# K pages and weights on one DMA queue, V pages on another, in a two-layer decode kernel

## The chip, the cores and the metric

The kernel runs on one core of one Trainium2 chip. The metric is the device time of one launch in microseconds (us), the median of several runs. Times inside an execution come from one profiled execution, taken by the hardware profiler, and are counted from the start of its span.

## What is computed

One token passes through two identical layers, each an attention block and a gated feed-forward block with residuals. The weights and caches of both layers are the same tensors, so the second layer reads them again. In short:

```python
W = 4096                                            # window: last 4096 of 32768 positions
q = (layernorm(x) @ wq)                             # 640 -> 32 heads x 192
scores = einsum("bhqd,bhkd->bhqk", q, k[-W:]) * 192 ** -0.5
x = x + einsum("bhqk,bhkd->bhqd", softmax(scores), v[-W:]) @ wo
y = layernorm(x)
x = x + (silu(y @ w1) * (y @ w3)) @ w2              # 640 -> 1536 -> 640
# and the same four lines once more
```

All data are bf16. Each head has its own K and V, so one head's window is 4096 x 192 elements, 1536 KB of K and as much of V.

## The kernel before

**Pages and slots.** All large data pass through one arena in on-chip memory (`arena`), cut into 16 slots (`NSLOT`) of 128 partitions x 6144 elements, 1536 KB each. One slot holds one page: a head's K window, a head's V window, a fifth of wq, or a part of wo, w1, w3 or w2.

**The list of loads.** The list `loads` (lines 147 to 172) is written out before anything runs. For each layer it holds five wq pages (`q`); then, for step i from 0 to 41, the V page of head number i - 10 and the K page of head number i, where these exist (`LEAD` is 10); then six entries for wo (`o`), which are 8 transfers, and four for the feed-forward weights (`fa` to `fd`). So the first ten K pages stand alone, then V and K alternate, and the last ten V pages stand alone. Heads go in four blocks of 8 (`HB`); their order is `ORDER`, other in the second layer than in the first. 13 K pages of the first layer (`RETAIN`) keep their slots and are not loaded again in the second layer.

**Who issues.** `refill` (line 174) takes entries off the list while a slot is free and issues their transfers at line 181, all on SP's queue (`nc.sync`). `done` (line 186) gives a page's slot back and calls `refill`. Both run while the program is being written: a transfer's place in the program is right behind the matmuls that were the last to read the slot it goes into, and `pin` keeps that order on each engine. An engine runs its instructions in the order of the program. The transfer waits for those matmuls and, as the semaphores go, for the landing of an earlier transfer. In all, 64 V pages, 51 K pages and 41 transfers of weights go this way. One small load, the input `xb` (line 75), is issued on ACT's queue before.

**One step of the attention** (`attention`, from line 407). Step i first takes V page i - 10 (`v_page`: 16 matmuls into `o_ps`), then K page i (`k_page`: two in-place transposes on DVE at line 262, then 12 matmuls into `s_ps`; a retained K page is not transposed again). PE takes these strictly in this order. ACT and the other engines do the following around blocks:

- before a block's first K page, `build_w` copies the block's q into `wst` with two copies on ACT (line 249) and two on POOL (line 251)
- after a block's last K page, `softmax_head`: the maximum on DVE (lines 274 to 283), `tb` on ACT (line 284), a transpose on DVE, the exp on ACT (line 289), a transpose on DVE (line 292)
- two steps later, `softmax_place`: five copies on ACT and three on DVE into `ptm` (line 302), which the V matmuls of the block read
- after the first V page of the next block, `combine`: a copy on ACT (line 321), two pairs of matmuls, and three operations on DVE that end in `otd`

**After the attention**, `wo_proj` multiplies `otd` by wo (96 small matmuls into `y_ps`), `y_to_residual` adds the result to x (from line 208), `layernorm` follows (from line 191), and `ffn` computes gate (`g_ps`), up (`u_ps`), silu and the product with w2. All matmuls carry line 72, the line of the helper `mm`. The last instruction is the store of `ob` (line 443).

Of the kernel before, what the change touches and what calls it, by code (L numbers as in the profile page):

```python
# [40 lines left out]
def kernel(  # L41
# [13 lines left out]
    nc = tc.nc  # L55
# [11 lines left out]
    def pin(ins):  # L67
        tc.keep_in_program_order(ins)
        return ins
# [104 lines left out]
    def refill():  # L174
        while free and loads:
            key, parts = loads.pop(0)
            s = free.pop(0)
            home[key] = s
            for off, n, src in parts:
                dst = arena[:, s * PGW + off:s * PGW + off + n] if off is not None else keep[:]  # L180
                pin(nc.sync.dma_start(out=dst, in_=src))  # L181

    def page(key):
        return arena[:, home[key] * PGW:home[key] * PGW + PGW]
# [1 line left out]
    def done(key):  # L186
        free.append(home.pop(key))
        refill()
# [218 lines left out]
    def attention(layer):  # L407
# [27 lines left out]
        wo_proj(layer)  # L435

    refill()
    ob = cst.tile([P, NCH], BF16, name="ob")
    for layer in range(2):
# [34 lines left out]
```

## Time and profile before

| what | value |
|---|---|
| median of 3 runs | 542.88 us (542.79 to 543.05) |
| profiled execution, its time | 548.4 us |
| profiled execution, its span | 546.6 us |
| bytes moved | 224.34 MB, mean 410 GB/s |
| SP's queue | 22608 packets, 223.98 MB |
| ACT's queue | 144 packets (`xb`) |
| mean granted TensorE clock | 0.668 of full speed |
| 0 to 280 us | 419 GB/s, DMA busy share 1.00 |
| 280 to 334 us | 381 GB/s, DMA busy share 0.96 |
| 334 to 541 us | 417 GB/s, DMA busy share 1.00 |

PE is TensorE's matmul row, PEld its weight loads, DVE is VectorE, ACT is ScalarE, POOL is GpSimd, SP is SyncE. A "q" behind an engine's name (SPq) stands for its sequencer, which issues transfers. Rows of groups give the line, engine, operation and the names written and read; rows of a timeline begin with start and duration in us. The chain is the work that ended last, followed back from the last instruction: at each step to what released it.

### The profile page before, as it was taken

What the parts mean: (1) busy time and instruction counts of PE and PEld (TensorE: products, weight loads), DVE (VectorE), ACT (ScalarE), POOL (GpSimd) and SP (SyncE); (2) the same over time, 40 slices, a digit from 0 to 9 for tenths busy, and PEclk for the clock granted to TensorE, in tenths of its full rate; (3) what the DMA queues carried; (4) which work ended last, traced back from release to release, by engine and by line L of the source; (5) the groups of instructions that cost most, each with busy time, mean ns of one, the idle gap of its engine ahead of it and who ended that gap; (6) DMA issues with size and microseconds to landing.
All of it is one profiled execution on the core that took longest, in us unless ns stands there. A gap on an engine that the chain in (4) does not pass through costs nothing.

```text
span 546.6 us, 5673 instructions
## 1 busy us (share of the span) xinstructions
PE 288.2 (53%) x2400; PEld 119.9 (22%) x2400; DVE 222.9 (41%) x262; ACT 41.9 (8%) x107; POOL 13.2 (2%) x50
## 2 busy tenths in 40 slices
PE   2355455555564655743544356767465566553544
PEld 1111122222221222211222122333121222221211
DVE  2189755565446654410012057234524744530011
ACT  1100200020001100010001010211001100020000
POOL 5000000000000000000000000000000000000000
PEclk9579595667665776555556558896866766565656
DMA  8999999999999999999999989999999999999993
GB/s 353 430 420 428 421 427 424 424 423 424 426 424 423 424 427 422 423 418 428 417 389 397 370 355 419 424 426 422 425 421 426 423 427 427 423 425 423 420 415 156
DMA packets 22777, 224.34 MB, mean 410 GB/s; under 512 B 2784, under 2 KB 3168, under 8 KB 5472
## 3 DMA queue, kind: packets, MB, share of 16 engines
q1 hardware_dynamic: 22608, 223.98, 98.3%
q8 instruction: 19, 0.31, 0.2%
q14 instruction: 6, 0.05, 0.0%
q10 hardware_dynamic: 144, 0.00, 0.0%
HBM read 223.97 MB, written 0.00 MB: 410 GB/s over the span
## 4 chain that ended last, share of the span: by engine, by line
DMA 79%; PE 11%; DVE 6%; ACT 1%; issue 1%; SPq 1%; POOL 0%; ACTq 0%; DVEq 0%
DMA arena<-in_A_k_cache_dram 54%; DMA arena<-in_A_v_cache_dram 9%; DMA arena<-in_A_wo_dram 7%; PE s_ps L72 7%; DMA arena<-in_B_w_dram 5%; DVE arena L262 4%; DMA arena<-in_A_wq_dram 4%; PE o_ps L72 3%; PE y_ps L72 1%; SPq L181 1%; PE q_ps L72 1%; ACT w L289 0%; DVE t L274 0%; ACT ptm L302 0%; DVE w L292 0%
## 5 line engine op out<-in xcount | busy, mean ns | idle before, releaser
L72 PE MATMUL s_ps<-arena,wst 128*32 128x512 bf16 x768 | 164.0, 523 | 154.5 <-DVE arena L262 149.1
L262 DVE STREAM_TRANSPOSE arena<-arena 128x1536 uint32<-128x1536 uint32 x102 | 174.8, 1753 | 110.7 <-DMA arena<-in_A_k_cache_dram 108.8
L72 PE MATMUL o_ps<-arena,ptm 128*16 128x384 bf16 (+1 forms) x1024 | 129.3, 457 | 34.7 <-DMA arena<-in_A_v_cache_dram 33.6
L72 PEld LDWEIGHTS <-wst 128*32 128x32 bf16 x768 | 54.8, 115 | 248.5 <-issue 205.0
L72 PEld LDWEIGHTS <-ptm 128*16 128x16 bf16 (+1 forms) x1024 | 48.9, 106 | 76.5 <-issue 60.6
L325 DVE RECIPROCAL rl<-rl_ps 128x1 f32<-128x1 f32 x8 | 1.3, 168 | 62.0 <-PE rl_ps L72 62.0
L284 ACT ACTIVATE tb<-m 32x32 f32<-32x32 f32 x8 | 1.8, 228 | 307.4 <-DVE m L281 307.4
L72 PE MATMUL y_ps<-arena,otd 128*1 128x320 bf16 x192 | 16.8, 448 | 16.2 <-DMA arena<-in_A_wo_dram 16.2
L72 PE MATMUL q_ps<-arena,xs 128*32 128x384 bf16 x160 | 13.9, 500 | 20.3 <-DMA arena<-in_A_wq_dram 19.0
L274 DVE TENSOR_REDUCE t<-s_ps 64x1 f32<-64x512 f32 x8 | 5.5, 683 | 34.4 <-PE s_ps L72 34.4
L302 ACT COPY ptm<-w 32x128 bf16<-32x128 bf16 x40 | 16.2, 405 | 28.7 <-PE o_ps L72 26.4
L72 PEld LDWEIGHTS <-xs 128*32 128x32 bf16 x240 | 9.2, 123 | 40.2 <-issue 31.3
L209 DVE CAST w<-y_ps 128x320 bf16<-128x320 f32 x4 | 2.0, 491 | 37.8 <-PE y_ps L72 37.8
L251 POOL COPY wst<-qt_sb 32x48 bf16<-32x48 bf16 x16 | 6.2, 385 | 406.0 <-PE s_ps L72 236.8
L234 DVE CAST w<-q_ps 128x768 bf16<-128x768 f32 x2 | 1.9, 958 | 31.4 <-ACT w L232 31.4
L72 PEld LDWEIGHTS <-otd 128*1 128x1 bf16 x192 | 6.5, 101 | 26.5 <-issue 22.4
L292 DVE STREAM_TRANSPOSE w<-w 64x512 bf16<-64x512 bf16 x8 | 5.6, 704 | 7.2 <-ACT w L289 7.2
L321 ACT CAST w<-o_ps 128x384 bf16<-128x384 f32 x8 | 3.8, 478 | 52.1 <-PE o_ps L72 51.9
L72 PE MATMUL u_ps<-arena,xs 128*32 128x384 bf16 x40 | 4.2, 508 | 6.4 <-DMA arena<-in_B_w_dram 6.4
L72 PE MATMUL st_ps<-xsq,onesD 128*128 128x12 f32 x8 | 2.3, 367 | 9.2 <-DVE xsq L191 9.2
L375 DVE CAST w<-u_ps 128x384 bf16<-128x384 f32 x2 | 1.1, 558 | 14.6 <-PE u_ps L72 14.6
L249 ACT COPY wst<-qt_sb 32x48 bf16<-32x48 bf16 x16 | 6.4, 398 | 4.3 <-DVE qt_sb L242 4.0
(69 smaller groups left out, 86.7 us busy)
## 6 DMA issues: line engine op xcount, KB each, us to landing
arena<-in_A_v_cache_dram SPq DMA_DIRECT2D x64, 1536.0 KB, 29.5
arena<-in_A_k_cache_dram SPq DMA_DIRECT2D x51, 1536.0 KB, 29.5
arena<-in_A_wq_dram SPq DMA_DIRECT2D x10, 1536.0 KB, 10.9
arena<-in_A_wo_dram SPq DMA_DIRECT2D x6, 1440.0 KB, 15.6
arena<-in_B_w_dram SPq DMA_DIRECT2D x4, 1536.0 KB, 14.4
arena<-in_A_wo_dram SPq DMA_DIRECT2D x4, 960.0 KB, 16.9
arena<-in_A_wo_dram SPq DMA_DIRECT2D x6, 480.0 KB, 14.1
arena<-in_B_w_dram SPq DMA_DIRECT2D x2, 960.0 KB, 14.4
```

Source lines behind the costliest of these rows:

```text
L72: return pin(nc.tensor.matmul(*a, **k))
L181: pin(nc.sync.dma_start(out=dst, in_=src))
L209: pin(nc.vector.tensor_copy(out=y_sb[:, 320:640], in_=y_ps[1][:, 0:320]))
L234: pin(nc.vector.tensor_copy(out=q_rep[par][:], in_=src))
L249: pin(nc.scalar.copy(out=dst, in_=src))
L251: pin(nc.gpsimd.tensor_copy(out=dst, in_=src))
L262: pin(nc.vector.transpose(x[:, w * sp:w * (sp + 1)].bitcast(U32), x[:, w * sp:w * (sp + 1)].bitcast(U32)))
L274: pin(nc.vector.reduce_max(out=t0[:, 0:1], in_=s_ps[0:64, :], axis=AX.X))
L284: pin(nc.scalar.mul(out=tb[32:64, :].rearrange("p (a z) -> p a z", a=4), in_=mb, mul=-SCALE))
L292: pin(nc.vector.transpose(et[:], e[:]))
L302: pin((eng.copy if eng is nc.scalar else eng.tensor_copy)(out=dst, in_=src))
L321: pin(nc.scalar.copy(out=o_sb[:, 0:384], in_=o_ps[:, 0:384]))
```

## The change

V pages are issued from ACT's DMA queue. K pages and all weights stay on SP's. The list of loads, its order, the slots and everything else are as they were; only the engine that issues an entry is chosen by its kind.

```diff
             for off, n, src in parts:
                 dst = arena[:, s * PGW + off:s * PGW + off + n] if off is not None else keep[:]
-                pin(nc.sync.dma_start(out=dst, in_=src))
+                pin((nc.scalar if key[0] == "v" else nc.sync).dma_start(out=dst, in_=src))
```

A V page's issue now stands in ACT's program, at the same place relative to the matmuls: behind what ACT was given before them, ahead of what it is given after.

## The prediction

> **What bounds the kernel now.** I read the page first: busy shares, the slices, the chain of what ended last. Then the waits of the DMA-issuing sequencer, then the timelines and the chain piece by piece at three places: the full stream, the end of layer 0's attention, the end of the kernel.
>
> ```profile
> PE 288.2 (53%) x2400; PEld 119.9 (22%) x2400; DVE 222.9 (41%) x262; ACT 41.9 (8%) x107; POOL 13.2 (2%) x50
> DMA  8999999999999999999999989999999999999993
> DMA 79%; PE 11%; DVE 6%; ACT 1%; issue 1%; SPq 1%; POOL 0%; ACTq 0%; DVEq 0%
> arena<-in_A_v_cache_dram SPq DMA_DIRECT2D x64, 1536.0 KB, 29.5
> arena<-in_A_wo_dram SPq DMA_DIRECT2D x6, 1440.0 KB, 15.6
> ```
>
> From the top: the engines' busy time, the DMA engines in 40 slices, the chain, and two groups of loads with us from issue to landing. No engine is over 53% busy, the 16 DMA engines are at 90% or more in nearly every slice, and the chain is 79% transfers. So transfers bound the kernel, and a change of queue can act in two ways only: by leaving the DMA engines without work, or by changing the order in which bytes land.
>
> ```profile
> SPq L181 <- DMA arena<-in_A_v_cache_dram: 175.4, 57, 3.6
> SPq L181 <- PE o_ps L72: 36.0, 20, 3.9
> SPq L181 <- DMA xb<-in_A_x_dram: 2.7, 1, 2.7
> ```
>
> Those are SP's waits (total us, times, longest); the next rows are its timeline (start, us, what).
>
> ```profile
> 130.47 0.33 SPq L181 DMA_DIRECT2D arena<-in_A_v_cache_dram  x1
> 134.16 0.33 SPq L181 DMA_DIRECT2D arena<-in_A_k_cache_dram  x1
> 137.89 0.33 SPq L181 DMA_DIRECT2D arena<-in_A_v_cache_dram  x1
> ```
>
> In the full stream SP issues one page per 3.70 us, and a page lands 29.5 us after its issue: 29.5/3.70 = 8 loads in flight. SP is not waiting for a slot there but for the landing of the load eight issues earlier. The row with xb matters most: an issue on SP waited for the landing of xb, which ACT had issued. So the eight places are shared by both queues, and the change doesn't deepen the stream.
>
> **Parts with no price.** 64 issues of 0.33 us (21 us) leave SP. SP's time is hidden behind landings, so nothing is gained. ACT gets 64 issues; its one issue of before (xb) took 0.395 us, so 25 us on an engine that is 8% busy. What matters is that ACT now waits. Queued behind a V issue are build_w's copies, tb, the exp, the placing copies and combine's copy, and PE and DVE wait for those. The worst place is a block's softmax. ACT did tb at 112.42 us; in program order it now stands behind the V issue that SP made at 130.47, so 18.1 us late, and the next block's build_w copies stand behind the one of 137.89. The next K page is then done at about 137.9 + 0.8 (copies) + 2.7 (PE) = 141.4, and the load that takes its slot was issued at 141.59 in before. Late by a microsecond or two, it costs nothing while seven other loads (25.8 us) are in flight. I take zero; without that cover it is the hold rival below.
>
> **The order of bytes.** The trace of before has two queues at work once. xb was issued on ACT at 0.74 us and landed at 7.07; the first wq page, issued on SP at 0.75, landed at 6.88. xb is 1.2 KB; served first it would have been there long before. It lasted as long as the 1536 KB beside it: packets of the two queues are taken in turn. So I let a V page and an SP page that are in flight together share the DMA engines evenly. In the full stream the pair lands when it did before, and nothing is lost.
>
> *End of layer 0's attention.* 13 K pages are kept, so three slots are left and few loads are in flight. Three pieces of the chain (start, us, what), then SP's timeline.
>
> ```profile
> 200.66 22.22 DMA arena<-in_A_k_cache_dram
> ...
> 222.97 3.45 DVE arena L262 x2
> ...
> 231.38 0.78 ACT w L289 x2
> ```
>
> ```profile
> 230.50 1.59 SPq L181 DMA_DIRECT2D arena<-in_A_v_cache_dram  x2
> ```
>
> The last K page lands at 222.88, ahead of a V page that was issued later. Sharing with that V page, it lands one page later, 3.70 us, at 226.6. From its landing run DVE's transposes, PE's 12 matmuls, the V page after them, and the next V load at 230.50 (7.6 us). On ACT that load also stands behind the block's exp, which ends at 232.16 (9.3 us after the K page). A load needs 6.13 us from issue to landing even on idle queues (the first one, 0.75 to 6.88), so the page that landed at 237.68 lands at 226.6 + 9.3 + 6.13 = 242.0: a hole of 4.3 us. If ACT's sequencer issues it ahead of the waiting exp, 226.6 + 7.6 + 6.13 = 240.3: 2.7 us. I take **4.3**, because every wait of ACT shown before stands in its order; everything behind it is a chain of transfers and moves with it. The trace has an ACTq row at L289 and at L302: the sequencer itself stops for waits. The Trainium skill (Advanced Engine Details and Errata, Sequencer and Instruction Queues) says that engine instructions are pushed into a queue and wait there while the sequencer reads on; by that the hole would be the smaller one and the sum 1.6 us less. Only the profile of the change can show which.
>
> *End of the kernel.* Here wo's 8 transfers (7680 KB, 5 pages' worth) follow the last ten V pages, and the slots are free. On one queue they wait their turn; on two they share with the V pages that the end of the attention is waiting for. SP's timeline and PE's:
>
> ```profile
> 483.14 26.23 SPq L181 DMA_DIRECT2D arena<-in_A_wo_dram  x8
> ```
>
> ```profile
> 509.02 1.46 PE L72 MATMUL o_ps<-arena,ptm 128*16 128x384 bf16 x16 [2.25 <-DMA arena<-in_A_v_cache_dram]
> ```
>
> The last V page lands at 508.97 (PE starts it at 509.02), the last big weight at 541.0 (the chain's piece "523.08 17.91 DMA arena<-in_B_w_dram"). The 32 us between them hide everything after the attention. Behind the last V page, with all weights there, stand: its matmuls and combine up to otd, 509.0 to 512.6, 3.6; 96 wo matmuls at 16.8/192 us, 8.4; residual and layernorm, 528.45 to 532.00, 3.55; gate 1.56; from the first up matmul to the first of w2, 535.21 to 539.82, 4.6; 24 w2 matmuls at the same price, 2.1; the end to ob, 1.2. Sum **25.0 us**: 7 us of cover.
> How far do the V pages fall back? Each of the last seven lets one wo transfer in when the load eight before lands; its bytes flow 6.13 - 3.70 = 2.43 us later, then the two take turns. By the time the last V page is down, six wo transfers (5760 KB) and a third of the seventh (480 KB) have passed it: 6240/1536 x 3.70 = 15.0 us. That is the upper bound; the lower is 0, if wo's issues find no free slot because consumption lags behind the ACT holds. The rows have SP waiting for landings there, not for slots, so I stay near the upper end and take one page off for the lag: **11.3 us**.
> The end: 508.97 + 4.3 + 11.3 + 25.0 = 549.6, where ob was ready at 543.19: **+6.4 us**. By the transfers alone it would be +4.3; with the full 15.0 it is +10.1; with the smaller hole and no falling back, +2.7.
>
> The sum is made on the profiled execution (span 546.6, time 548.4). The median of the runs shown is 542.88, 5.5 us less; I carry the difference over: 542.9 + 6.4 = **549.3**.
>
> One rule speaks of this very change. The Trainium skill (DMA: Bandwidth & Descriptors, Issuing engines are not separate DMA queues) says that issuing from several engines only saves the sequencer's issue time. By it the sum would be zero and the time 542.9; it says nothing of who lands first, which is where I see the cost.
>
> **The rivals.**
> *Served in order of issue (10%).* If the DMA engines take the two queues' loads as they were issued, the K page isn't late and wo passes nobody. What is left is the V load behind the exp: issued at 232.2 for 230.50. It had to be out 2.43 us before the landing at 233.99, at 231.55, so 0.6 us: **543.5**, no change. It decides if xb's late landing had another cause, such as its 128 tiny packets.
> *A faster stream (8%).* Twice in the full stream a page takes 5.2 us in place of 3.70 (SP's issues at 29.07 and 34.26, at 400.23 and 405.48). If a second queue has packets ready where one stalls, that is 3.0 us: **539.9**. The weak stretch, 280 to 334 us at 381 GB/s, can't gain: no V page is issued from 250.3 to 329.9. It needs the in-order service above as well.
> *All of wo passes (13%).* If more than eight loads are in flight (counters for each queue), all five pages go first, 18.5 us: 508.97 + 4.3 + 18.5 + 25.0 - 543.19 = +13.6, **556.5**. The xb row speaks against it.
> *The holds empty the stream (5%).* If each of the six later block starts holds PE one page beyond the loads in flight, 6 x 3.7 = 22 us: **565**. 18.1 + 7.4 + 3.5 us of hold against 29.5 in flight is just short of it.
>
> **How the numbers follow.** The forecast has 64%, from 545.5 (+2.7) to 553 (+10.1). The range goes to the first rival below and the third above, 543.4 to 556.6; left out are the faster stream, the holds and some of the edges. About 0.2% (1.1 us) is what a measurement of this kernel tells from no change. Faster 8%, same 10%, slower 82% (64 + 13 + 5).
>
> **What would show it.** 64 pages, 100.7 MB, on a second queue. The last K page of layer 0 landing a page late against its V neighbours, and a hole in the DMA of 3 to 4 us near 232. build_w's ACT copies in the full stream tens of microseconds behind the softmax's place in before, with DMA still at 9. The last V page near 525, wo pages landed before it, and PE, not DMA, in the chain of the last 20 us. I am wrong if K and V pages land in the order of their issue, if more than eight loads are in flight, or if DMA shows holes at the block starts.

## The result and the profile after

The changed kernel took **549.03 us** (median of runs from 547.55 to 549.99) where the kernel before took 542.88. The ratio is 1.0104, with a 95% interval of 1.0088 to 1.0119. It is slower by about 6 us. The profiled execution of the change took 547.55 us and its span is 545.8 us.

That execution can't be held against the profile shown before the prediction, whose 548.4 us lie 5.5 us above the median of their own kernel. The unchanged kernel was therefore profiled once more (first experiment below). That second profile has a time of 543.11 and a span of 541.3; it is the one compared here, and it is called "before" from now on. First the change: engines, DMA slices, GB/s per slice, the two queues, the chain, and three groups of loads with the us from issue to landing.

```profile
PE 260.6 (48%) x2400; PEld 111.3 (20%) x2400; DVE 221.1 (41%) x262; ACT 42.0 (8%) x107; POOL 13.1 (2%) x50
...
DMA  8999999999999999979999999999999999999994
GB/s 350 428 425 423 426 424 425 423 424 424 425 424 425 424 425 424 412 302 425 413 386 411 425 416 416 425 424 424 426 423 422 427 424 426 423 422 422 423 420 187
...
q1 hardware_dynamic: 13392, 123.31, 54.3%
q10 hardware_dynamic: 9360, 100.67, 44.0%
...
DMA 78%; PE 10%; DVE 7%; ACT 2%; issue 2%; ACTq 0%; SPq 0%; POOL 0%; DVEq 0%
...
arena<-in_A_v_cache_dram ACTq DMA_DIRECT2D x64, 1536.0 KB, 17.3
arena<-in_A_k_cache_dram SPq DMA_DIRECT2D x51, 1536.0 KB, 26.6
...
arena<-in_A_wo_dram SPq DMA_DIRECT2D x6, 1440.0 KB, 11.5
```

Then the same slices of the second profile of before:

```profile
DMA  8999999999999999999999999999999999999994
GB/s 352 429 423 423 427 423 424 425 424 425 423 424 425 426 422 424 429 418 425 420 397 417 424 399 426 425 422 424 426 421 428 424 424 423 426 426 422 421 417 176
```

The V pages went to the second queue (q10, 100.67 MB), and transfers still bound the kernel. What moved is the order: a V page is now there 17.3 us after its issue, a K page after 26.6, where both took 29.5. In only one place do the slices differ by much: the 18th, 232 to 246 us, moved 302 GB/s in place of 418, the only 7 in the DMA row. From 220 to 240 us the changed kernel lacks 4.4 us of transfers against a rate of 425 GB/s (summed from the trace's transfers; before lacks 0.2 us there). That is nearly the whole difference between the two profiled executions, whose spans are 4.5 us apart.

The waits of SP's sequencer (total us, times, longest) show that the places in flight are shared, as they were for xb: SP, which issues no V page any more, waits mostly for V pages to land. Counted from issue to landing, this trace never has more than eight loads in flight, both queues together.

```profile
SPq L181 <- DMA arena<-in_A_v_cache_dram: 230.1, 22, 46.3
SPq L181 <- DMA arena<-in_A_k_cache_dram: 101.7, 20, 14.8
```

**At the end of layer 0's attention.** Two pieces of the chain after the change (start, us, what), and the two that answer to them before:

```profile
209.64 17.45 DMA arena<-in_A_k_cache_dram
227.18 3.45 DVE arena L262 x2
```

```profile
199.13 23.83 DMA arena<-in_A_k_cache_dram
222.97 0.03 issue
...
223.06 3.45 DVE arena L262 x2
```

The last K page lands at 227.08 in place of 222.97, 4.1 us later. It also goes out 10.5 us later, but that alone wouldn't make it late: the K page ahead of it lands at 219.68, and by then the last one has been in flight for 10 us. With the DMA engines to itself it would need 3.70 us more and land at about 223.4 (an estimate). It takes 7.40, and a V page that went out after it, at 213.87, lands ahead of it, at 226.60. Next ACT's timeline after the change, and SP's before, both where the next V load goes out (the x2 joins it with the one behind it):

```profile
235.28 0.68 ACT L289 ACTIVATE w<-s_ps,nbt 64x512 bf16<-64x512 f32 x1 [0.35 <-DVE nbt L286]
235.40 0.82 ACTq L181 DMA_DIRECT2D arena<-in_A_v_cache_dram  x2
```

```profile
230.34 1.26 SPq L181 DMA_DIRECT2D arena<-in_A_v_cache_dram  x2
```

The issue stands at 235.40 in place of 230.34. It went out 0.12 us after the exp had begun: the sequencer stood behind the exp while that waited, but not until it ended at 235.96. From the K page's landing to this issue it takes 8.3 us in place of 7.4. The load lands 6.1 us later, at 241.50, where the page ahead of it landed at 234.00: 7.5 us between two landings that lie 3.70 apart in the stream. The sum closes: 4.1 (K page) + 0.9 (exp) less 1.3 (before, the load had 7.42 us to land and needs 6.1) gives 3.7 us, and 241.50 lies 3.74 us after the 237.76 of before.

**At the end of the kernel.** PE's timeline after the change, then before:

```profile
522.24 1.46 PE L72 MATMUL o_ps<-arena,ptm 128*16 128x384 bf16 x16 [5.70 <-DMA arena<-in_A_v_cache_dram]
...
525.24 4.79 PE L72 MATMUL y_ps<-arena,otd 128*1 128x320 bf16 x96
...
539.21 0.45 PE L72 MATMUL y_ps<-arena,htd 128*1 128x320 bf16 x8 [0.86 <-DVE htd L390]
540.22 0.71 PE L72 MATMUL y_ps<-arena,htd 128*1 128x320 bf16 x13 [0.57 <-DMA arena<-in_B_w_dram]
```

```profile
503.05 1.46 PE L72 MATMUL o_ps<-arena,ptm 128*16 128x384 bf16 x16 [2.23 <-DMA arena<-in_A_v_cache_dram]
```

The last V page lands at 522.20 in place of 503.00, far behind its old place in the stream. All 96 wo matmuls then run in one go: five of wo's eight transfers landed before that V page, and the last lands at 526.89, while they run. And yet PE arrives at w2 at 539.21 and waits 0.57 us there, until 540.22, for the last weights: transfers still end last, with a cover of about 1 us.

### The profile page after: what moved, and what is told of

The parts are those of the page before. It is cut to its first block, busy times and chain, and to the rows that moved or that the text cites. A ratio compares the mean times of both kernels' runs of the same rounds, so it can differ in the third digit from the quotient of the medians.

```text
span 545.8 us, 5688 instructions
## 1 busy us (share of the span) xinstructions
PE 260.6 (48%) x2400; PEld 111.3 (20%) x2400; DVE 221.1 (41%) x262; ACT 42.0 (8%) x107; POOL 13.1 (2%) x50
## 3 DMA queue, kind: packets, MB, share of 16 engines
q10 hardware_dynamic: 9360, 100.67, 44.0%
## 4 chain that ended last, share of the span: by engine, by line
DMA 78%; PE 10%; DVE 7%; ACT 2%; issue 2%; ACTq 0%; SPq 0%; POOL 0%; DVEq 0%
DMA arena<-in_A_v_cache_dram 36%; DMA arena<-in_A_k_cache_dram 26%; DMA arena<-in_A_wq_dram 7%; PE s_ps L72 6%; DMA arena<-in_B_w_dram 5%; DVE arena L262 4%; DMA arena<-in_A_wo_dram 4%; PE o_ps L72 2%; ACT ptm L302 1%; PE y_ps L72 1%; PE q_ps L72 1%; DVE t L274 1%; ACTq L181 0%; SPq L181 0%; DVE r L279 0%
## 5 line engine op out<-in xcount | busy, mean ns | idle before, releaser
L72 PE MATMUL s_ps<-arena,wst 128*32 128x512 bf16 x768 | 150.4, 494 | 162.6 <-DVE arena L262 105.1
L72 PE MATMUL o_ps<-arena,ptm 128*16 128x384 bf16 (+1 forms) x1024 | 107.3, 416 | 56.8 <-DMA arena<-in_A_v_cache_dram 35.8
L72 PEld LDWEIGHTS <-wst 128*32 128x32 bf16 x768 | 52.6, 112 | 245.8 <-issue 209.8
L72 PEld LDWEIGHTS <-ptm 128*16 128x16 bf16 (+1 forms) x1024 | 41.0, 101 | 93.6 <-issue 57.2
L72 PE MATMUL q_ps<-arena,xs 128*32 128x384 bf16 x160 | 14.7, 519 | 25.4 <-DMA arena<-in_A_wq_dram 24.1
L286 DVE STREAM_TRANSPOSE nbt<-tb 64x32 f32<-64x32 f32 x8 | 1.6, 203 | 48.6 <-ACT tb L284 48.0
L72 PE MATMUL y_ps<-arena,otd 128*1 128x320 bf16 x192 | 13.4, 418 | 6.4 <-DMA arena<-in_A_wo_dram 6.4
L302 DVE COPY ptm<-w 32x128 bf16<-32x128 bf16 x24 | 6.2, 260 | 6.6 <-PE o_ps L72 5.5
L331 DVE SCALAR_TENSOR_TENSOR om<-ot_ps,rl,mask 128x192 bf16<-128x192 f32 x8 | 3.3, 418 | 7.9 <-PE ot_ps L72 7.8
## 6 DMA issues: line engine op xcount, KB each, us to landing
arena<-in_A_v_cache_dram ACTq DMA_DIRECT2D x64, 1536.0 KB, 17.3
arena<-in_A_k_cache_dram SPq DMA_DIRECT2D x51, 1536.0 KB, 26.6
arena<-in_A_wo_dram SPq DMA_DIRECT2D x4, 960.0 KB, 14.7
```

The lines of the kernel that those rows point to most:

```text
L72: return pin(nc.tensor.matmul(*a, **k))
L302: pin((eng.copy if eng is nc.scalar else eng.tensor_copy)(out=dst, in_=src))
L331: pin(nc.vector.scalar_tensor_tensor(out=om[:], in0=ot_ps[:], scalar=rl[:], in1=mask[:].unsqueeze(2).broadcast_to([P, 16, 12]), op0=ALU.mu ...
```

## The experiments

**Theories.** Mine: the time is lost at the end of layer 0's attention, because V pages pass the kept K pages that PE waits for; what stands behind ACT's instructions adds a little; the fall-back of V at the end adds 2.1 us. The rivals: ACT's holds alone, or the passing at the end, make most of it.

All edits but two are to line 181 alone. Unless a minus line says otherwise, the plus line stands in place of the change's `pin(...)` line. "Hole" is the lack of transfers from 220 to 240 us, reckoned as above. In the table K is the landing of the last kept K page of layer 0 and V the landing of the first V load that goes out more than 1 us after it.

| kernel | ratio to before | K | V | hole |
|---|---|---|---|---|
| before, again (e0) | 1.0001 [0.9992, 1.0010] | 222.97 | 237.76 | 0.2 |
| the change | 1.0104 [1.0088, 1.0119] | 227.08 | 241.50 | 4.4 |
| V on ACT in layer 0 alone (e1) | 1.0121 [1.0096, 1.0147] | 227.80 | 242.87 | 5.7 |
| V on ACT in layer 1 alone (e2) | 0.9994 [0.9985, 1.0002] | 223.04 | 237.82 | 0.1 |
| all on ACT (e3) | 1.0032 [1.0022, 1.0042] | 223.40 | 238.21 | 0.8 |
| last 16 V of layer 0 on SP (e4) | 1.0002 [0.9993, 1.0011] | 222.84 | 237.63 | 0.2 |
| 8 V of layer 0 alone on ACT (e5) | 1.0048 [1.0033, 1.0063] | 224.70 | 238.43 | 1.5 |
| last 8 K of layer 0 on ACT too (e6) | 1.0023 [1.0013, 1.0033] | 222.84 | 237.76 | 0.8 |
| last 2 K of layer 0 on ACT too (e11) | 1.0060 [1.0045, 1.0076] | 223.03 | 231.89 | 3.2 |
| K alone on ACT (e10) | 1.0130 [1.0114, 1.0146] | 228.00 | 241.52 | 4.2 |
| V alone on SP (e7) | 1.0251 [1.0237, 1.0265] | 227.80 | 241.39 | 4.3 |

### Before, once more (e0)

```diff
+                pin(nc.sync.dma_start(out=dst, in_=src))
```

> The kernel before, once more, for a second profile of it. The profiled execution of before took 548.4 us, 5.5 us over the median of its runs, and its trace lacks about 7 us of bytes between 270 and 330 us. If that stretch is part of the kernel, it is there again and the span is near 546. If it was a feature of that one execution, the span is near 541 and the stretch runs at the 424 GB/s of the rest. The time should be within 0.2% of 542.9 either way.

Measured: 543.16 us, and a profile with a span of 541.3. The stretch at 381 GB/s between 280 and 334 us isn't in it: there this profile has 415. So that stretch belonged to one execution and is no part of the kernel, and the 5.5 us that the prediction carried as a difference between profile and median were that execution's own. In every later run the time is 1.7 to 1.9 us over the span, but for e7's 2.8.

### V on ACT in layer 0 alone (e1), in layer 1 alone (e2)

```diff
+                pin((nc.scalar if key[0] == "v" and key[1] == 0 else nc.sync).dma_start(out=dst, in_=src))
```

> Only the first layer's V pages go on ACT's queue. My theory: most of the cost is one hole at the end of the first layer's attention (3.8 us in the trace of after), because the last kept K page shares the DMA engines with V pages; the hole is there again, so 3.8 to 5 us more than before, 546.7 to 548. Rival, wo passes the last V pages at the end of the kernel: no change here, 542.9. Rival, two queues or the holds of ACT cost a little everywhere: about half of the 6.1 us, 546.

```diff
+                pin((nc.scalar if key[0] == "v" and key[1] == 1 else nc.sync).dma_start(out=dst, in_=src))
```

> Only the second layer's V pages go on ACT's queue. My theory: no hole, since no K page is kept there and eight loads are in flight; but the last V page lands some 13 us later than in before, and the end is a tie between PE and the last weights, so 0 to 2.5 us more, 543 to 545.4. Rival, wo passing is the whole cost: 549. Rival, a little everywhere: 546.

Measured: 549.25 us with layer 0 alone, 1.2 us above what I had expected, and 542.88 with layer 1 alone. The whole cost is in layer 0. The stretch from 220 to 245 us of e1 (start and end, us, busy us of PE, PEld, DVE, ACT, POOL, clock, DMA share, GB/s):

```profile
220.00:245.00 25.00, 13.31 (x108) 5.57 (x109) 11.24 (x18) 3.49 (x9) 0.00 (x0) 0.64 0.83 329
```

and of before:

```profile
220.00:245.00 25.00, 13.09 (x119) 5.20 (x114) 7.82 (x16) 3.50 (x9) 0.00 (x0) 0.64 1.01 421
```

DMA moved 329 GB/s in place of 421, 5.5 us of the 25, and the K page and the V load are late in the same way as in the change.

In e2 the passing at the end is there in full, and costs nothing. PE's timeline:

```profile
516.31 1.46 PE L72 MATMUL o_ps<-arena,ptm 128*16 128x384 bf16 x16 [5.43 <-DMA arena<-in_A_v_cache_dram]
...
534.21 1.73 PE L72 MATMUL y_ps<-arena,htd 128*1 128x320 bf16 x19 [0.85 <-DVE htd L390]
```

The last V page lands at 516.27, 13.3 us after its place in before. PE reaches w2 at 534.21, the last weights land at 535.35 (before 535.45). My 2.1 us at the end falls; that the passing happens does not.

### All transfers on ACT's queue (e3)

```diff
+                pin((nc.scalar).dma_start(out=dst, in_=src))
```

> Every transfer of pages goes on ACT's queue, none on SP's (but the store at the end). The holds of ACT are there in full, but one queue keeps the order of bytes of before. My theory: the order of bytes is the cost, so 542.9, at most 0.6 us more for the V load that stands behind the last exp of the first layer. Rival, the holds of ACT cost the time: 546 to 549 or more, with holes in the DMA at the block starts.

Measured: 545.12 us. There is one queue again, so nothing is passed, while ACT stands in front of every load. The page's rows of PE and DMA in 40 slices:

```profile
PE   0040554642572556644545456670475033730184
...
DMA  8999999999999999999999999999999999999994
```

PE stands idle in whole slices, while DMA stays at 9: the holds are real and the loads in flight cover them. What stays is 1.7 us (0.32%), more than the 0.6 that I had allowed and far from the 6 of the change. At the end of layer 0's attention the V load goes out 8.6 us after the K page, in place of 7.4, which leaves a hole of 0.8; most of the rest lies between 270 and 330 us, where this kernel lacks 3.3 us of transfers and before 1.9.

### The late V pages back on SP (e4), the late K pages on ACT (e6)

```diff
+                pin((nc.scalar if key[0] == "v" and not (key[1] == 0 and key[2] < 16) else nc.sync).dma_start(out=dst, in_=src))
```

> As the change, but the first layer's last 16 V pages, the ones beside and behind the last kept K pages, go on SP's queue again. My theory: the hole comes from those few pages alone, so it is gone and with it nearly all of the cost, 542.9 to 544. Rival, the delay is built up over the whole first layer (V pages run ahead of K pages from the start): a good part stays, 546 or more.

```diff
+                pin((nc.scalar if key[0] == "v" or (key[0] == "k" and key[1] == 0 and key[2] < 8) else nc.sync).dma_start(out=dst, in_=src))
```

> As the change, but the first layer's last eight K pages go on ACT's queue too, so that they and the V pages beside them are in one queue in their old order; ACT is held by all of them. My theory: the last K page is on time and the hole shrinks to what the V load behind the exp makes, as with everything on ACT: 544 to 545.5. Rival, the holds of ACT make the hole: 548 or more.

Measured: 543.18 and 544.42 us. Two repairs from opposite sides. Both put the last K pages of layer 0 and their V neighbours on one queue, and in both the K page lands at 222.84 and the hole of the change is gone, though 48 V pages of 64 (e4) and all of them (e6) still go through ACT. What e6 keeps is the exp: its load goes out at 231.47 in place of 230.34, and a hole of 0.8 us. The stretch of e4, then of e6:

```profile
220.00:245.00 25.00, 13.49 (x119) 5.36 (x116) 7.80 (x16) 3.50 (x9) 0.00 (x0) 0.64 1.01 421
...
220.00:245.00 25.00, 12.01 (x115) 4.87 (x108) 7.82 (x16) 3.49 (x9) 0.00 (x0) 0.64 1.00 414
```

That is 421 and 414 GB/s, beside 421 before and 329 in e1. With this the cause is shown and not argued: the cost is there when V pages share the DMA engines with the last kept K pages from another queue, and it goes when they don't.

### Only the eight V pages beside the last K pages (e5)

```diff
+                pin((nc.scalar if key[0] == "v" and key[1] == 0 and 8 <= key[2] < 16 else nc.sync).dma_start(out=dst, in_=src))
```

> The counterpart: only eight V pages of the first layer, numbers 16 to 23, which land beside the last K pages, go on ACT's queue; the other 56 stay on SP's. My theory: the hole is there as in the change, 547 to 549. Rival, the delay is built up over the whole layer: 543 to 545.

Measured: 545.65 us, below what I expected. These eight pages are the ones that travel beside the last K pages, and they make a little under half of the cost. The last K page lands 1.7 us late and not 4.1. From the one before it, it lies 7.40 us, two pages' time. That by itself shows no sharing, since before has the same 7.40 (215.57, 222.97), with a V page between the two in one queue; here too a V page that went out earlier lands in between (221.95). The step is as long as in before and starts 1.7 us later, where in the change it starts 4.1 us later. The lateness of layer 0's last seven K pages against before (us, by landings):

| | 7th from the end | 6th | 5th | 4th | 3rd | 2nd | last |
|---|---|---|---|---|---|---|---|
| the change | 12.0 | 11.1 | 8.7 | 7.4 | 4.1 | 4.1 | 4.1 |
| e5 | 14.7 | 12.4 | 11.0 | 7.3 | 3.6 | 1.7 | 1.7 |

In layer 0 of the change the first 25 K pages land 11 to 26 us late, while V pages, with which they share from the first one on, land up to 49 us early. Toward the end V's lead is used up (the V pages just ahead of the last K page and just behind it land within 0.5 us of their time in before), and the K pages catch up. What is left of the lag at the last K page is the cost. That this is about one page, as I had put it, is where the change happens to stand.

### The last two K pages on ACT (e11)

```diff
+                pin((nc.scalar if key[0] == "v" or key in (("k", 0, 6), ("k", 0, 7)) else nc.sync).dma_start(out=dst, in_=src))
```

> As the change, but the last two K pages of the first layer go on ACT's queue too, so that only these two are in one queue with the V pages beside them. If the hole comes from these two pages alone sharing with their neighbours, it shrinks as with all eight of the last K pages there: about 544.4. If it comes from the lag that the whole stream of K pages has by then, these two are late all the same and 546 to 549 remain.

Measured: 547.0 us, between the change and e6. The two moved pages are on time, at 214.45 and 223.03. Now the third from the end, alone on SP's queue, is the one that is passed: it lands at 218.41, 10.2 us late and behind its successor. PE takes pages in order, so slots come free late; the next V load goes out at 225.77 and lands at 231.89, 5.2 us after the landing ahead of it. The hole moves some 9 us forward and is still 3.2. So it doesn't take the last page: a page ahead of it, on the queue that is passed, has much the same effect.

### One kept page fewer, before (e8) and after (e9)

```diff
-RETAIN = (0, 1, 2, 3, 4, 5, 6, 7, 8, 11, 14, 18, 21)
+RETAIN = (0, 1, 2, 3, 4, 5, 6, 7, 8, 11, 14, 18)
```

> The kernel before with 12 K pages kept in place of 13 (head 21 is loaded again in the second layer). One page more is moved, 3.7 us, and four slots are left at the end of the first layer's attention in place of three: 542.9 + 3.7 = 546.6. If four slots remove some of the small losses at the layer's end (1.7 us in the second profile of before), 545.

> The change with 12 K pages kept in place of 13. My theory: the hole needs a stream that is one page short of work when the last K page is a page late; with a fourth slot one more load is in flight, and of the 4.4 us hole at most 0.7 us are left. So 0 to 1 us over the kernel before with 12 kept, near 547, and less than the change itself in spite of the page more. Rival, the hole comes with the late K page whatever is in flight: 549 + 3.7 = 552.7.

Both load one page more; e8 has the loads of before, e9 those of the change. Measured: 546.37 (1.0057 [1.0043, 1.0071]) and 549.2 us (1.0107 [1.0091, 1.0123]), so the change costs 2.8 us with four slots free at that place, where it costs 6 with three. I had expected 1 at most. The fourth slot lets one load more go out ahead of the K page's landing, but that is another V page (at 221.18), which shares with the K page as well. The K page lands at 229.28, 6.35 us later than in e8 (222.93). The hole is 3.4 us. A slot more halves the cost here and doesn't remove it.

### The queues the other way round: K alone on ACT (e10), all but V on ACT (e7)

```diff
+                pin((nc.scalar if key[0] == "k" else nc.sync).dma_start(out=dst, in_=src))
```

> As the swapped kernel (+13.7 us), but the weights stay on SP's queue with the V pages; only K pages go on ACT's. My theory: 8.1 of the 13.7 us came after the last transfer, because wo and the feed-forward weights on the other queue passed the last V pages and PE ended last; with V pages and weights in one queue that is gone, and the hole of the first layer stays: 546.5 to 549. Rival, K pages on ACT's queue cost this themselves: 555 or more.

```diff
+                pin((nc.sync if key[0] == "v" else nc.scalar).dma_start(out=dst, in_=src))
```

> The queues are swapped: V pages on SP's queue, K pages and weights on ACT's. The last K page shares the DMA engines with V pages as in the change, but the V load behind it no longer stands behind the exp. My theory: the late K page remains, 3.7 to 4.2 us, and the part of the exp goes, 0.8 to 1.7 us: 546.5 to 548. Rival, the exp in front of the V load makes most of the hole: 544 or less.

Measured: 550.31 and 556.81 us. In both the V load behind the last K page goes out on SP, 7.1 and 7.4 us after that page, so no exp stands in front, and the hole is there all the same: 4.2 and 4.3 us. That holds the exp to a small part. Both missed my numbers, e10 by 1.3 us and e7 by 8.8. In e10 another 2.3 us of transfers are lacking around 320 us, which I didn't follow further. In e7 the end of the kernel comes on top. Its chain:

```profile
505.59 26.15 DMA arena<-in_A_v_cache_dram
531.79 1.30 PE o_ps L72 x16
...
534.17 4.36 PE y_ps L72 x54
```

The last V page lands at 531.75, 28.7 us after its place in before, with the hole in it. All weights are there by 541.78, and PE, with 18.1 us of work behind that V page, is done at 549.9: some 8 us that nothing covers. In e10, where V and wo share a queue, the last V page lands at 509.56 and the last weights end the kernel again. So the passing at the end, free in the change, costs once it goes a little further. How much of e7's 28.7 us are packets taken in turn, and how much ACT's copies (PE waited 27.87 us for line 302 at 514.07, while ACT stood behind issues of wo), these two runs don't tell.

## Why the prediction was right, and where it was not

The direction, the size and the place were right: slower, 549.03 for 549.3, by bytes that land in another order. Taken by its own steps:

- **Transfers bound the kernel, eight places in flight for both queues.** Right: DMA is 78% of the chain, and SP waits for V pages that ACT issued.
- **64 issues and ACT's holds at no price.** Nearly right: e3 has holds on every load, whole slices of idle PE, and DMA at 9. It costs 1.7 us in all, some 0.6 of it the exp that I had priced in the next step; where the rest comes from isn't shown.
- **Queues are served in turn.** Right. It was read from one row of xb. The change shows it directly: from 212 to 222 us, with K and V pages in flight, SP's queue moved 2.11 MB and ACT's 2.13 (summed from the trace's transfers).
- **End of layer 0's attention, 4.3 us.** Right in mechanism, and too small. K page late: predicted 3.70, measured 4.1 (4.8 in e1). Exp: predicted 1.7 us, measured 0.9 to 1.3, between the two cases, since the issue went out when the exp began and not when it ended. The hole: 4.4 us in the profiled execution of the change, which is the fastest of its runs; 5.7 in e1. With the end at zero, the 6 us of the medians are probably nearly all this hole; no execution at the median was traced. The K page's lateness isn't one page by rule, it is what is left of a lag that had reached 26 us.
- **End of the kernel, +2.1 us.** Wrong, it is 0 (e2). Two terms in it failed in opposite directions. The V page falls back 13.3 us (e2), not 11.3: of the page taken off for the lag, about half should have stayed. And the chain behind it was put at 25.0 us, 21.7 of them up to the first w2 matmul; up to there it takes 17.9 in e2, and in e7 18.1 to the very end. Its largest error is wo: 8.4 us for 96 matmuls, priced by a row in which they waited for pieces of wo; with wo there they took 5.73 (e2) and 4.79 (the change). So the cover, 7 us as written and 9.2 in the sum itself (508.97 + 25.0 against ob at 543.19), was in truth some 14 (32.4 us in before from the last V page to the last weights, less 17.9 in e2 from the V page to w2), and 13.3 of fall-back just fit in. Transfers, and not PE as I had named for a sign, still end the chain.
- **The carried difference of 5.5 us** between profile and median: the sum needed it only to be set upon the median, which was sound, but it was one execution's disturbance.

So against the medians the total came out right partly by luck, because two errors cancel: the hole was put 1.5 to 2 us too small, the end 2.1 us too large. Of the rivals, service in order of issue is refuted by the last K page, which a V page issued 4.2 us after it passes; the faster stream by full-stream slices that stay at 423 to 428 GB/s (before 422 to 429); the holds by e3; and all of wo passing by the eight loads in flight, and by wo's last three transfers, which land after the last V page (522.37, 525.70 and 526.89; 522.20). Only e7's time looks like that one's, and it got there in another way.

Two rules of the Trainium skill were weighed in the prediction. DMA: Bandwidth & Descriptors, section Issuing engines are not separate DMA queues, says that transfers of all issuing engines interleave on the same DMA engines and that several issuers save only issue time. The first half agrees with these runs (2.11 and 2.13 MB of the two queues side by side, as above); by the second the kernel would be unchanged, and the ratio of 1.0104 decides against leaving it there. Advanced Engine Details and Errata, section Sequencer and Instruction Queues, has engine instructions wait in a queue while the sequencer reads on. Here the issue behind the exp didn't go out while the exp waited: it left 0.12 us after the exp began (235.40, 235.28), so this trace doesn't show it running ahead.

**What stays open.** The times of the change vary more: it ran from 547.55 to 549.99 us and e1 from 548.34 to 553.02, while before stayed within 542.2 to 544.7, but for its first profiled execution (548.4). That the hole's size is what varies is read from two traces (4.4 and 5.7 us), and why the lag that is left should differ between executions was not found. The split of e7's loss, and the 2.3 us of e10 near 320 us, stay open too. No version tried beat the kernel before; e2 and e4 equal it.

## What to carry to other kernels

Where transfers are the bound, a second queue doesn't add bandwidth, it reorders bytes: ask which page will be passed, whether somebody waits for exactly that one, and how many loads are in flight there to cover it. Pages that one consumer takes in a fixed order belong on one queue, above all where slots run short. And a chain timed while it waited for data is longer than the same chain once the data are there, so cover reckoned from it comes out too small.

## What was unexpected of the hardware

The wo matmuls cost less the later they came. In before, 96 of them between 506.5 and 522.5 us were busy for 8.68 us at a granted clock of 0.50; back to back they took 5.85 at 0.59 (e2; its window holds 104), 4.83 at 0.71 (the change; 100) and 3.95 at 0.88 (e7; 104). Duration times clock is 3.4 to 3.5 in the last three and 4.3 in the first, so most of the gain is the clock. These rows don't show why it was granted; the three had waited longer for their V page just before.

A single profile can mislead by 1%: the first of before lacks 6.3 us of transfers between 270 and 330 us, the second 1.9. And whole slices of idle PE beside a DMA at 9 (e3) went with a loss of only 1.7 us.
